# Zeros on TensorE in the first microseconds, one transfer for omega, and a place in the queue for the weight sums

## The chip, the cores and the metric

The kernel runs on one core of a Trainium2 chip. The metric is the device time of one execution in microseconds (us), as the median of three runs; lower is better. One further execution was recorded by the hardware profiler, and all rows below come from it.

## The reference

The program is random-feature attention, followed by two feed-forward blocks.

```python
def phi(x):                     # x: (4, 8, 576, 64), omega: (128, 64)
    h = einsum('bhsd,md->bhsm', x * scale, omega) - sum(x*x)/2
    return exp(h - max(h)) / sqrt(128)
q_p, k_p = phi(q), phi(k)
kv, z = einsum('bhsm,bhsd->bhmd', k_p, v), sum(k_p over s)
attn = (q_p @ kv) / (q_p @ z + 1e-6)          # -> x: (2304, 512)
y = ((x @ w_a) * (x @ w_b)) @ w_out           # 512 -> 1536 -> 512
out = maximum(y @ w_in, 0)**2 @ w_out2        # 512 -> 2048 -> 512
```

Inside `phi`, the term with the sum of squares is the same for every feature of a row and drops out against the maximum, so the kernel does not compute it.

## The kernel before

**Stages.** The prologue loads omega twice over, one copy above the other, turns it through TensorE against an identity matrix (`ident`), scales it and keeps it as `OMZ` and `OM`. Then *lanes* of small steps make the attention of the first 512 rows, batch 0, heads in pairs: a transfer brings a pair's rows (`kn` for k, `qn` for q), TensorE turns them (`ps_t`), ScalarE copies them out (`S`), TensorE multiplies with `OMZ` (`ps_p`), VectorE takes the extreme of each row (`nm`), ScalarE exponentiates (`kp`, `qp`). For k the result meets `V` on TensorE (`ps_kv`); for q it is turned once more (`ps_qt`), multiplied with the sums (`ps_n`), divided (`den`, `xh`) and turned into the columns of `x`. Rows 512 to 575 of each batch are called tails (`kt`, `qt`, `VT`, `ps_kt`). In fp32 each product of the program stands as two matmul records in the trace.

From about 40 us on the first feed-forward block runs in nine *passes* over blocks of 256 tokens. Passes 0 to 5 handle one block and half of the twelve 128-wide slices `f` of the hidden layer each (`PASSES`), with operands of 256 columns; passes 6, 7 and 8 handle two blocks and all slices, 512 columns at once, and are called wide. For each `f` a pass yields three units: product a (`wa`), product b (`wb`), and the output product (`y`) of an earlier slice. After product b the gate is formed: ScalarE scales a into `a_s`, VectorE multiplies b in, ScalarE casts the high part to fp32r and VectorE subtracts it from `a_s` for the low part; the two go to `gs` in narrow passes and to `g_mid` in wide passes 6 and 7. Between units the rest of the attention goes on as side lanes (`SIDES`).

**The weight sums.** Passes 6 and 7 take their later slices in pairs, by a Strassen-like scheme with seven products (`sP`, `sR`) for eight (`pair`). It needs sums of the weights: the generator `t_made(f)` (L282) adds the two parts of slice f's weights over 1,024 columns (`full`), makes four differences of 256 columns, and cuts each of the four results in a high part (ScalarE) and a low part (VectorE), in a `cut` tile, of which there are two. A transfer on SyncE's queue puts each `cut` into `t_d` in DRAM, from where `t_load` fetches it as `tsum` or `tz`. Ten slices are made, 6 to 11 and then 2 to 5, one step of the generator per unit of pass 6 (`t_work`).

**What sets the order.** The program is traced in the order in which it is written, and a scheduler then sets each engine's queue in advance: an instruction may go up the queue when its inputs and its memory are ready earlier. `tc.issue_after(x)` keeps what is traced in its block behind x in the queue of x's engine, without any wait for x to finish. Each engine works its queue strictly in order, so an instruction that waits holds up all behind it. Because of the scheduler's freedom, sums that pass 6 asks for can stand in the queues far ahead of pass 6.

`tail_turn` (L399) with `phi_wide` (L409) is the path of the tails; `load_split` and `step` cut the weights into parts, and `later_n` counts steps until one put-off part is issued.

## Time and profile before

| | us |
|---|---|
| median of 3 runs | 977.52 |
| lowest and highest run | 977.36, 978.56 |
| the profiled execution | 979.28 |
| its span, first to last instruction | 977.2 |

The profiled execution is 1.76 us over the median, and 2.1 us of it lie around the span. The profile gives, for each engine, when it was busy, when it was idle and what ended the idle time. TensorE appears as PE (matmuls) and PEld (weight loads), VectorE as DVE, ScalarE as ACT, GpSimd as POOL, and the queue on which SyncE issues transfers as SPq. A row of the timeline gives the start, the time to the end of the last of its instructions, and their number. The column PEclk is the granted share of TensorE's clock; it reads 1.00 in all windows shown, the first one included, and whether matmuls of one form take the same time in two stretches has to be read from their durations.

### The profile page before, as it was taken

How to read it: one execution, taken by the hardware profiler on the slowest of the kernel's cores; microseconds unless marked ns; L12 is line 12 of the kernel's file. 1: busy time of each engine (PE TensorE's matmuls, PEld its weight loads, DVE VectorE, ACT ScalarE, POOL GpSimd, SP SyncE). 2: the span in 40 equal slices, each digit the busy share in tenths (PEclk: the TensorE clock that was granted, in tenths of full speed). 3: DMA queues.
4: the chain of work that ended last, by engine and by line, in shares of the span. 5: the costliest groups of instructions: out<-in, count | busy, mean ns of one | idle time of the engine just before them, and what ended most of it. 6: DMA issues, size and time to landing. Idle time of an engine off the chain costs nothing.

```text
span 977.2 us, 18208 instructions
## 1 busy us (share of the span) xinstructions
PE 961.5 (98%) x6625; PEld 898.0 (92%) x6625; DVE 728.8 (75%) x1688; ACT 551.5 (56%) x1310; POOL 28.8 (3%) x54
## 2 busy tenths in 40 slices
PE   7999999999999999999999999999999999999998
PEld 6799998999998889889998888899999999999998
DVE  3888689887787865565456989789787347988794
ACT  5876566666655643253433544677676565555561
POOL 4000100000000000000000000000000000000000
PEclk9999999999999999999999999999999999999999
DMA  8656976655775365346547989246666869944301
GB/s 207 208 176 204 307 234 212 226 179 182 218 213 167 130 199 171 113 153 188 170 143 254 350 304 339 66 160 207 216 227 220 317 250 357 390 135 146 115 17 50
DMA packets 121961, 198.39 MB, mean 203 GB/s; under 512 B 28944, under 2 KB 84752, under 8 KB 119440
## 3 DMA queue, kind: packets, MB, share of 16 engines
q1 hardware_dynamic: 120336, 195.65, 60.5%
q0 software_dynamic: 1536, 1.58, 0.6%
q8 instruction: 53, 0.87, 0.4%
q14 instruction: 36, 0.29, 0.1%
HBM read 136.90 MB, written 60.29 MB: 202 GB/s over the span
## 4 chain that ended last, share of the span: by engine, by line
PE 81%; DVE 7%; DMA 5%; ACT 4%; issue 2%; SPq 0%; DVEq 0%; ACTq 0%
PE y L811 13%; PE abw L786 9%; PE oY L1478 8%; PE pY L1294 7%; PE ab L786 7%; PE oX L1478 5%; PE oW L1478 5%; PE sP L919 5%; PE pW L1294 4%; PE sR L919 3%; PE ps_n L638 3%; PE ps_kv L571 3%; PE ps_p L415 3%; PE ps_p L490 2%; DMA raw<-in_moe_w_b_dram 2%; PE ps_qt L628 2%
## 5 line engine op out<-in xcount | busy, mean ns | idle before, releaser
L786 PE MATMUL abw<-x_all,W 128*128 128x512 f32 x432 | 104.1, 392 | 0.0
L786 PEld LDWEIGHTS abw<-x_all,W 128*128 128x128 f32 x432 | 80.0, 188 | 15.7
L786 PE MATMUL ab<-x_all,W 128*128 128x256 f32 x576 | 84.9, 290 | 0.4 <-ACT W L226 0.4
L786 PEld LDWEIGHTS ab<-x_all,W 128*128 128x128 f32 x576 | 74.0, 189 | 1.7 <-ACT W L226 0.6
L811 PE MATMUL y<-g_mid,wo 128*128 128x512 f32 x288 | 75.1, 401 | 0.0
L811 PE MATMUL y<-gs,wo 128*128 128x256 f32 x432 | 66.5, 290 | 0.0
L811 PEld LDWEIGHTS y<-g_mid,wo 128*128 128x128 f32 x288 | 51.9, 188 | 10.1
L811 PEld LDWEIGHTS y<-gs,wo 128*128 128x128 f32 x432 | 56.6, 189 | 1.0 <-DVE wo L227 0.2
L1294 PE MATMUL pY<-W,M 128*128 128x384 f32 x228 | 44.1, 336 | 0.4 <-ACT F L1312 0.4
L499 ACT COPY c<-ps_p 128x256 f32<-128x256 f32 x76 | 27.7, 372 | 28.6 <-PE ps_p L490 28.1
L501 DVE CUSTOM_DVE_ANT_0 c<-ps_p,c 128x128 f32<-128x128 f32 x152 | 38.2, 285 | 7.5 <-ACT c L499 6.8
L786 PE MATMUL ab<-x,W 128*128 128x256 f32 x288 | 42.5, 288 | 0.0
L1442 ACT CAST W<-F 128x384 fp32r<-128x384 f32 x57 | 29.1, 513 | 22.9 <-PE oX L1478 11.0
L1478 PE MATMUL oX<-W 128*128 128x256 f32 x351 | 41.9, 276 | 0.0
L1478 PEld LDWEIGHTS oX<-W 128*128 128x128 f32 x351 | 40.8, 188 | 0.0
L1294 PEld LDWEIGHTS pY<-W,M 128*128 128x128 f32 x228 | 39.8, 188 | 1.0 <-ACT F L1312 0.9
L1320 ACT ACTIVATE F<-F 128x384 f32<-128x384 f32 x48 | 24.7, 518 | 26.9 <-DVE F L1315 26.7
L1478 PE MATMUL oY<-W 128*128 128x256 f32 x315 | 38.6, 277 | 0.0
L786 PEld LDWEIGHTS ab<-x,W 128*128 128x128 f32 x288 | 37.6, 191 | 0.1
L506 ACT ACTIVATE qp<-c,nm 128x128 f32<-128x128 f32 x88 | 31.0, 397 | 11.3 <-DVE nm L501 10.8
L1478 PEld LDWEIGHTS oY<-W 128*128 128x128 f32 x315 | 37.1, 188 | 0.0
L419 DVE TENSOR_REDUCE nm<-ps_p 128x4 f32<-128x512 f32 (+1 forms) x44 | 24.7, 564 | 14.9 <-PE ps_p L415 14.7
(287 smaller groups left out, 2408.7 us busy)
## 6 DMA issues: line engine op xcount, KB each, us to landing
wo<-wo_d SPq DMA_DIRECT2D x60, 512.0 KB, 3.9
s_d<-F SPq DMA_DIRECT2D x24, 768.0 KB, 4.7
tsum<-t_d SPq DMA_DIRECT2D x26, 512.0 KB, 4.0
t_d<-cut SPq DMA_DIRECT2D x40, 256.0 KB, 2.9
raw<-in_moe_w_out_dram SPq DMA_DIRECT2D x32, 256.0 KB, 5.2
raw<-in_moe_w_in_dram SPq DMA_DIRECT2D x16, 512.0 KB, 6.4
raw<-in_moe_w_a_dram SPq DMA_DIRECT2D x12, 512.0 KB, 3.8
raw<-in_moe_w_b_dram SPq DMA_DIRECT2D x12, 512.0 KB, 5.8
```

Of the source, the lines that this page charges most:

```text
L415: state["proj"] = nc.tensor.matmul(ps[:, 2 * x:2 * x + 2].rearrange("p h m -> p (h m)"), lhsT=s, rhs=OMZ.rearrange("p h m -> p (h m)"), st ...
L499: nc.scalar.copy(out=c, in_=ps[:, :, 1, :])
L501: nc.vector.tensor_tensor_reduce(out=c[:, x, :], in0=ps[:, x, 0, :], in1=c[:, x, :], scale=1.0, scalar=3.0e38, op0=ALU.add, op1=ALU.min, a ...
L506: nc.scalar.activation(out=dst[:, 2 * n + x, :], in_=c[:, x, :], func=ACTF.Exp, scale=-1.0, bias=nm[:, x:x + 1],)
L571: lambda h=h, j=j: nc.tensor.matmul(ps[:, h, :], lhsT=kp[:, 4 * h + j, :], rhs=V2[h][:, j] if odd else V[:, j, h, :], start=(j == j0), sto ...
L638: lambda x=x: nc.tensor.matmul(pn[:, x, :], lhsT=t["qT"][:, x % 2 * len(g) + x // 2, :], rhs=kv[:, x % 2, :], start=True, stop=True,)
L786: nc.tensor.matmul(ps, lhsT=wv[:, s_, kc, :], rhs=x[..., kc, m_, :], start=(kc == 0 and (s_, m_) == TERMS[0]), stop=(kc == KC - 1 and (s_, ...
L811: nc.tensor.matmul(y_part(pi, f, c), lhsT=wo[pi, f][:, s_, c * 128:(c + 1) * 128], rhs=g[:, m_, :],  start=(f == f0 and (wide or c % 2 == ...
L919: nc.tensor.matmul(ps[:, z], lhsT=b(z, s_, kk), rhs=a[:, kk, m_, :], start=(first and z == 0 and kk == 0 and (s_, m_) == TERMS[0]), stop=( ...
L1294: nc.tensor.matmul(ps[c][:, x, 0:TH], lhsT=w[:, s_, 128 * kk:128 * kk + 128], rhs=y[:, ai, kk, m_, :], start=((c, x) not in seen and kk == ...
L1442: ahead_of["cast"] = nc.scalar.copy(out=sop[:, 0], in_=src)
L1478: nc.tensor.matmul(tiles_of(p, t), lhsT=sops[n][:, s_, 128 * t:128 * t + 128], rhs=w[:, m_, :], start=(fresh and k == 0 and (t % 2 == 0 or ...
```

## The change

In the prologue, VectorE clears `OMZ` before `V` and `VT`, and casts it into the last 256 columns of the weight area `W`, where it serves as a block of zeros. `fill(n)` issues n matmuls of 128x256 zeros into a bank that nothing reads (`blank`): 8 ahead of omega's turning, 6 behind it, and 4 behind the turning of the first k rows. The first `ps_p` products are queued behind these. Omega comes by one transfer that reads it twice. The first tail's turning moves behind the second product of the first k rows. Every weight sum is queued behind the most recent gate: the addition of `full` behind the gate's VectorE subtraction, the casts into `cut` behind its ScalarE cast. So that the most recent gate is known, the wide passes now record it in `state["g"]` too. One put-off part of the first weights goes one step later (`later_n`).

```diff
@@ -239,7 +239,7 @@
         return state["g"][0] if at == "g" else at and state[at]
 
     waiting = []
-    later_parts, later_n = [], [9]
+    later_parts, later_n = [], [10]
     CAST_BEHIND = {("a", 6): "cast", ("a", 7): "S", ("a", 10): "g", ("a", 1): "S"}
     APART = {("a", 6), ("a", 10)}
 
@@ -285,10 +285,11 @@
 
         w = seg("W", 8192 * f, 2, 2, 512)
         full = top["full"].tile([128, 4, 256], F32, tag="full", name="full")
-        nc.vector.tensor_tensor(
-            out=full.rearrange("p (a r) n -> p a (r n)", a=2), in0=f32(w[:, :, 0]),
-            in1=f32(w[:, :, 1]), op=ALU.add,
-        )
+        with tc.issue_after(state["g"][1].ins):
+            nc.vector.tensor_tensor(
+                out=full.rearrange("p (a r) n -> p a (r n)", a=2), in0=f32(w[:, :, 0]),
+                in1=f32(w[:, :, 1]), op=ALU.add,
+            )
         yield
         for o, x, y in ((0, 2, 0), (2, 3, 2), (3, 3, 0), (1, 1, 3)):
             nc.vector.tensor_tensor(
@@ -298,7 +299,8 @@
             cuts = []
             for x in (n, n + 1):
                 c = top["cut"].tile([128, 2, 256], F32, tag="cut", name="cut")
-                nc.scalar.copy(out=c[:, 0].bitcast(F32R), in_=full[:, x])
+                with tc.issue_after(state["g"][0].ins):
+                    nc.scalar.copy(out=c[:, 0].bitcast(F32R), in_=full[:, x])
                 nc.vector.tensor_tensor(
                     out=c[:, 1].bitcast(F32R), in0=full[:, x], in1=c[:, 0], op=ALU.subtract
                 )
@@ -355,6 +357,16 @@
             for fn in fns[-2::-1]:
                 fn()
 
+    zero = area["W"][:, FA * 2048 - 256:FA * 2048]
+    blank = bank(7, [128, 512], "blank")[:, 0:256]
+
+    def fill(n):
+
+        for _ in range(n):
+            state["fill"] = nc.tensor.matmul(
+                blank, lhsT=zero[:, 0:128], rhs=zero, start=True, stop=True,
+            )
+
     def prologue():
         warm = ap2.tile([128, 1], F32, tag="den", name="warm", bufs=3)
         nc.vector.memset(warm, 0.0)
@@ -362,17 +374,23 @@
         make_identity(nc, ident)
         for t in V2:
             nc.scalar.copy(out=t[:, :, D:D + 1], in_=warm.unsqueeze(1).to_broadcast([128, 4, 1]))
-        nc.sync.dma_start(out=om[:, 0, :], in_=omega)
-        nc.sync.dma_start(out=om[:, 1, :], in_=omega)
-
-
-        nc.vector.memset(V, 1.0)
-        nc.vector.memset(VT, 1.0)
+        nc.sync.dma_start(out=om, in_=omega.unsqueeze(1).to_broadcast([M, 2, D]))
+
+
+        nc.vector.memset(OMZ, 0.0)
+        t = nc.vector.tensor_copy(out=zero, in_=OMZ.rearrange("p a m -> p (a m)"))
+        with tc.issue_after(t.ins):
+            t = nc.vector.memset(V, 1.0)
+        with tc.issue_after(t.ins):
+            nc.vector.memset(VT, 1.0)
         nc.vector.memset(VT[64:128, :, :, 0, :], 0.0)
         nc.vector.memset(VT[0:64, :, :, 1, :], 0.0)
-        nc.vector.memset(OMZ, 0.0)
+        fill(8)
         ps = at_bank([128, M], "ps_om")
-        nc.tensor.transpose(ps, om.rearrange("p a d -> p (a d)"), ident)
+        with tc.issue_after(state["fill"].ins):
+            t = nc.tensor.transpose(ps, om.rearrange("p a d -> p (a d)"), ident)
+        with tc.issue_after(t.ins):
+            fill(6)
 
         nc.scalar.mul(out=OMS, in_=ps, mul=-SCALE)
         for x in range(2):
@@ -411,11 +429,12 @@
         n = 2 * len(rows)
         nm = ap2.tile([128, n], F32, tag="nm", name="nm", bufs=4)
         ps = at_bank([128, n, M], "ps_p")
-        for x, s in enumerate(rows):
-            state["proj"] = nc.tensor.matmul(
-                ps[:, 2 * x:2 * x + 2].rearrange("p h m -> p (h m)"), lhsT=s,
-                rhs=OMZ.rearrange("p h m -> p (h m)"), start=True, stop=True,
-            )
+        with tc.issue_after(state["fill"].ins) if "proj" not in state else nullcontext():
+            for x, s in enumerate(rows):
+                state["proj"] = nc.tensor.matmul(
+                    ps[:, 2 * x:2 * x + 2].rearrange("p h m -> p (h m)"), lhsT=s,
+                    rhs=OMZ.rearrange("p h m -> p (h m)"), start=True, stop=True,
+                )
         nc.vector.tensor_reduce(out=nm, in_=ps, axis=AXX, op=ALU.min)
         for x in range(n):
             state["exp"] = nc.scalar.activation(
@@ -461,6 +480,12 @@
                 with tc.issue_after(state["proj"].ins):
                     for c in cols:
                         nc.tensor.transpose(ps[:, c], nat[:, c], ident)
+            elif "k" in self.at:
+                with tc.issue_after(state["fill"].ins):
+                    for c in cols:
+                        t = nc.tensor.transpose(ps[:, c], nat[:, c], ident)
+                with tc.issue_after(t.ins):
+                    fill(4)
             else:
                 together([lambda c=c: nc.tensor.transpose(ps[:, c], nat[:, c], ident) for c in cols])
             if self.wide:
@@ -525,7 +550,12 @@
                         in_=v[b, h0:h0 + 2, SM:S, :].rearrange("h t d -> t h d"),
                     )
         yield
-        st = tail_turn("k", b, g)
+        if state["n"] < 4:
+            yield
+            with tc.issue_after(state["proj"].ins):
+                st = tail_turn("k", b, g)
+        else:
+            st = tail_turn("k", b, g)
         yield
         yield
         kp = ap2.tile([128, 2, M], F32, tag="qp", name="kpt", bufs=2)
@@ -959,8 +989,7 @@
             outs(*pending.pop(0))
             g = top["g"].rearrange("p z h (t n) -> p t z h n", t=2)
             for t, e in enumerate((e1, e5)):
-                nc.scalar.copy(out=g[:, t, :, 0], in_=e)
-                nc.vector.tensor_tensor(
+                state["g"] = nc.scalar.copy(out=g[:, t, :, 0], in_=e), nc.vector.tensor_tensor(
                     out=g[:, t, :, 1], in0=e, in1=f32(g[:, t, :, 0]), op=ALU.subtract
                 )
             for z in range(2):
@@ -1041,8 +1070,7 @@
                 if len(pending) > 1:
                     outs(*pending.pop(0))
                 for c, a_s in a_ss:
-                    nc.scalar.copy(out=g[:, 0, c], in_=a_s)
-                    nc.vector.tensor_tensor(
+                    state["g"] = nc.scalar.copy(out=g[:, 0, c], in_=a_s), nc.vector.tensor_tensor(
                         out=g[:, 1, c], in0=a_s, in1=f32(g[:, 0, c]), op=ALU.subtract
                     )
                 for _ in range(2):
```

TensorE's queue at the program's start, before: omega's turning, the first k rows, the products with `OMZ`, the tail's turning (`ps_tt`).

```order
L375 MATMUL ps_om<-ident,om 128x128
L465 MATMUL ps_t_177<-ident,kn 128x128 x4
L415 MATMUL ps_p<-OMZ,S 128x256
L403 MATMUL ps_tt<-ident,kt 128x128
L415 MATMUL ps_p<-OMZ,S 128x256 x3
L415 MATMUL ps_p<-OMZ,T 128x256
```

The same place in the changed kernel:

```order
L366 MATMUL blank<-W 128x256 x8
L391 MATMUL ps_om<-ident,om 128x128
L366 MATMUL blank<-W 128x256 x6
L486 MATMUL ps_t_192<-ident,kn 128x128 x4
L366 MATMUL blank<-W 128x256 x4
L434 MATMUL ps_p<-OMZ,S 128x256 x2
L421 MATMUL ps_tt<-ident,kt 128x128
L434 MATMUL ps_p<-OMZ,S 128x256 x2
L434 MATMUL ps_p<-OMZ,T 128x256
```

Eighteen matmuls are new, and `ps_tt` stands one product later; the products themselves keep their order.

VectorE's queue in pass 3, where the first of the ten weight sums stands before (`c,nm`, `qT` and `den` belong to side lanes):

```order
L501 ISA c,nm<-ps_p,c 128x128
L501 ISA nm 128x1
L633 COPY qT<-ps_qt 128x512
L288 TENSOR_TENSOR full<-W 128x1024
L609 TENSOR_SCALAR den<-ps_n 128x4
```

The same place now:

```order
L526 ISA c,nm<-ps_p,c 128x128
L526 ISA nm 128x1
L663 COPY qT<-ps_qt 128x512
L1092 TENSOR_TENSOR a_s<-ab,a_s 128x256
L526 ISA c,nm<-ps_p,c 128x128
L526 ISA nm 128x1
L639 TENSOR_SCALAR den<-ps_n 128x4
```

The 1,024-column addition is gone from here, and the gate's multiplication (`a_s`) comes up. VectorE's queue in the changed kernel between two gates of pass 6, a place where no such row stood before in this number:

```order
L1093 TENSOR_TENSOR g_mid<-a_s,g_mid 128x256
L1092 TENSOR_TENSOR a_s<-abw,a_s 128x256
L295 TENSOR_TENSOR full<-full 128x256
L639 TENSOR_SCALAR den<-ps_n 128x4
L295 TENSOR_TENSOR full<-full 128x256
L1093 TENSOR_TENSOR g_mid<-a_s,g_mid 128x256
L295 TENSOR_TENSOR full<-full 128x256
L304 TENSOR_TENSOR cut<-full,cut 128x256
L295 TENSOR_TENSOR full<-full 128x256
L642 RECIPROCAL den<-den 128x4
```

All ten additions of `full` now stand here, behind the last gate of pass 5; before, seven of the ten stood ahead of the first gate of pass 6.

## Rows read from the trace of the kernel before

**Rows 1.** The page's first part: busy time, share of span, instructions.
```profile
PE 961.5 (98%) x6625; PEld 898.0 (92%) x6625; DVE 728.8 (75%) x1688; ACT 551.5 (56%) x1310; POOL 28.8 (3%) x54
```

**Rows 2.** Timeline of the start: start us, us, engine, line, instruction, count, idle before.
```profile
0.95 0.49 DVE L369 MEMSET V<- 128x520 f32 x1
1.19 0.42 SPq L366 DMA_DIRECT2D om<-in_omega_dram  x1
1.65 0.43 SPq L441 DMA_DIRECT2D kn<-in_k_dram  x1
...
5.00 1.11 PE L465 MATMUL ps_t<-ident,kn 128*128 128x128 f32 x4 [1.54 <-DMA kn<-in_k_dram]
...
6.15 0.58 ACT L468 COPY S<-ps_t 128x512 f32<-128x512 f32 x1 [1.62 <-PE ps_t L465]
...
6.79 1.22 PE L415 MATMUL ps_p<-OMZ,S 128*128 128x256 f32 x2 [0.68 <-ACT S L468]
...
8.02 2.77 PE L415 MATMUL ps_p<-OMZ,S 128*128 128x256 f32 x6
...
9.11 0.69 DVE L419 TENSOR_REDUCE nm<-ps_p 128x4 f32<-128x512 f32 x1 [4.25 <-PE ps_p L415]
...
9.84 1.14 ACT L421 ACTIVATE kp<-ps_p,nm 128x128 f32<-128x128 f32 x4 [1.31 <-DVE nm L419]
...
11.54 1.14 ACT L421 ACTIVATE kp<-ps_p,nm 128x128 f32<-128x128 f32 x4 [0.57 <-DVE nm L419]
...
12.50 0.51 PE L571 MATMUL ps_kv<-V,kp 128*128 128x65 f32 x2
12.56 0.64 ACT L421 ACTIVATE kpt<-ps_p,nm 128x128 f32<-128x128 f32 x2
...
12.96 0.34 PE L571 MATMUL ps_kv<-V,kp 128*128 128x65 f32 x2
...
14.57 0.87 ACT L468 COPY S<-ps_t 128x256 f32<-128x256 f32 x2
15.00 2.43 PE L415 MATMUL ps_p<-OMZ,S 128*128 128x256 f32 x10
```

**Rows 3.** Windows: stretch, length, busy time (instructions) by engine, PEclk, DMA share, GB/s.
```profile
core 0: us, PE busy (x) PEld busy (x) DVE busy (x) ACT busy (x) POOL busy (x), PEclk, DMA share, GB/s
0.00:15.00 15.00, 9.64 (x42) 7.74 (x42) 3.97 (x10) 7.01 (x23) 7.75 (x18) 1.00 0.91 230
34.00:42.00 8.00, 7.25 (x52) 6.12 (x50) 7.74 (x14) 7.62 (x21) 0.00 (x0) 1.00 0.84 263
160.00:180.00 20.00, 19.77 (x161) 18.81 (x160) 18.66 (x57) 12.40 (x33) 0.00 (x0) 1.00 0.69 228
175.00:287.00 112.00, 110.91 (x917) 107.23 (x917) 90.19 (x346) 75.38 (x233) 4.67 (x8) 1.00 0.66 202
287.00:404.00 117.00, 115.61 (x716) 99.85 (x716) 80.97 (x259) 54.52 (x160) 2.32 (x4) 1.00 0.52 168
```

**Rows 4.** Chain of waits: start us, us, what; a paired product, two sum transfers.
```profile
189.31 6.10 DMA t_d<-cut
...
295.53 4.15 DMA t_d<-cut
...
359.86 1.42 PE sP L919 x12
```

**Rows 5.** The sums' instructions: duration ns min/median/max, first and last start us.
```profile
L294 DVE TENSOR_TENSOR full<-full x40: 405/419/427, 180.6 to 330.7; 128x256 f32<-128x256 f32 x40
L301 ACT CAST cut<-full x40: 388/407/418, 181.8 to 339.4; 128x256 fp32r<-128x256 f32 x40
L302 DVE TENSOR_TENSOR cut<-full,cut x40: 404/419/426, 185.0 to 342.2; 128x256 fp32r<-128x256 f32 x40
L288 DVE TENSOR_TENSOR full<-W x10: 1216/1222/1226, 175.9 to 327.0; 128x1024 f32<-128x1024 f32 x10
```

**Rows 6.** The transfers of the sums (L308), from issue to landing.
```profile
DMA to landing us min/median/max: 2.0/2.9/6.1
```

## The prediction

> **What bounds the kernel now.** I read the page first, then windows of the stages that the change touches, then the timeline of the start, then the chain of waits. The page shows TensorE busy for 961.5 us of a span of 977.2 us, while VectorE has 728.8 us and ScalarE 551.5 us [rows 1]. So only 15.7 us of TensorE's time are idle, and a change can win in three ways: fewer idle microseconds, matmuls that take less time, or fewer matmuls. This change removes no matmul and adds eighteen. The windows say where idle time is [rows 3]: 5.4 us of the first 15 (15.00 less 9.64), 1.1 us of the 112 between 175 and 287 us (the end of the narrow passes, where seven of the ten weight sums are made), and 1.4 us of the 117 between 287 and 404 us (pass 6). The reader is to see that the start alone holds a third of all idle time.
>
> The timeline shows that the start is slow in a second way [rows 2]. The six matmul records at 8.02 us take 2.77 us, 0.46 each; ten records of the same form at 15.00 us take 2.43 us, 0.24 each. The pair of `ps_kv` at 12.50 us takes 0.51 us, the pair at 12.96 us 0.34. So TensorE runs at about half rate until some 12.7 us and then at full rate; I read the two as its levels of 1.2 and 2.4 GHz. The column of the granted clock does not tell them apart, since it reads 1.00 in the first window as everywhere [rows 3]. Before the rise TensorE had worked without a break since 6.79 us, after an idle gap of 0.68 us, that is for 5.9 us.
>
> **Part 1: zeros and omega.** VectorE's first large step, the clearing of `V`, starts at 0.95 us and takes 0.49 us for 520 columns [rows 2], so clearing 256 columns of `OMZ` takes some 0.25 us. The cast of 256 columns has no row; the nearest is a subtraction of 256 columns at 0.42 us [rows 5], which I take as its upper end. So the zeros are there at 0.95 + 0.25 + 0.42 = 1.6 us. A fill of 256 fp32r columns at full rate takes 1.42 us / 12 = 0.12 us [rows 4], at half rate 0.23. Eight end at 1.6 + 1.9 = 3.5 us. Omega is turned behind them, later than now, but is only needed by the first product at 6.79 us, which covers it with about 3 us. Six more fills end near 5.1 us. The first k rows land about 0.4 us sooner, since one transfer issue of 0.42 us ahead of theirs is gone; TensorE reaches them at 5.1 us at the soonest, against 5.00 now. The last four fills take 0.9 us beside a copy to `S` of 0.58 us, so at half rate they hold the first product by up to 0.3 us, at full rate by nothing. I put the first product at 6.9 us: a loss of 0.1, bounds 0 and 0.3.
>
> What comes back is the half rate behind it. If TensorE works without a break from 1.6 us and its clock rises after as long a stretch as now, it rises at 1.6 + 5.9 = 7.5 us in place of 12.7. I walk the chain of the first k rows on from there, first as if the clock were up by the first product. Two products are four records, 0.97 us; the reduction, which started at 9.11 us, starts near 7.9; it takes 0.69, and the exponentials of 1.14 us run from 8.6 to 9.8. The second reduction hides beside them. The next two sets of exponentials (1.14 and 0.64 us) are ScalarE's own work and end near 11.5, against 13.20 now (12.56 + 0.64). ScalarE then has a gap of 1.37 us before the next copies to `S` at 14.57 us, in which it mostly waits for `ps_kv` matmuls at half rate; at full rate they are nearly done when the last exponentials are. I leave 0.4 us of the gap, and after half of the 0.87 us of copies the next products start at 12.4 us, where they start at 15.00 now: 2.6 us sooner. With the whole gap left it is 1.7. With the clock up only at 7.5, 0.6 us of half rate stays ahead of the reduction, worth 0.3; together with the 0.1 above I take **2.2 us**.
>
> The Trainium skill, page "TensorE: Matmul & The Clock Gate", section "HAM oscillation — how this bites in real kernels", prices a slow stretch at half its length. By that rule the 5.9 us would be worth 3.0 us, and the total 0.8 us lower than mine; in this trace the exponentials of ScalarE lie between, and they do not get shorter. The same page, section "What's actually happening", says that the moment of the rise changes from run to run of one kernel; the three runs here differ by 1.2 us, which does not speak against it, and one profile cannot show it.
>
> From 15 us on every queue keeps its order up to pass 3, and transfers are issued as buffers come free, so the lead should be carried on. What would be late next is a transfer: in the first 15 us the DMA engines are busy at a share of 0.91 [rows 3], and the third load of k rows now stands behind the load of the output weights on SyncE's queue. That could take back some tenths. `ps_tt` and the put-off part of the first weights move by one step and cost nothing, since the two products and the exponentials cover them.
>
> **Part 2: weight sums.** One slice costs VectorE 1.22 + 4 x 0.419 + 4 x 0.419 = 4.57 us and ScalarE 4 x 0.407 = 1.63 us [rows 5]. Seven slices leave the stretch of 175 to 287 us: 32 us of VectorE's 90.2 and 11 us of ScalarE's 75.4. They go to the stretch of 287 to 404 us, where VectorE comes from 81.0 to some 110 or 113 of 117 us, 94 to 97%, and ScalarE from 54.5 to 66.
>
> In the first stretch TensorE is idle for 1.1 us in all. One idle wait there follows a transfer of a sum of 6.10 us [rows 4], for which ScalarE stands until a `cut` tile is free. The gain lies between 0 and 1.1 us; I take 0.7, since VectorE falls to about half load.
>
> In pass 6 behind a waiting sum stand gates, features and turned columns, on which TensorE's next products wait. Two rows bound the price of so full a VectorE [rows 3]. Between 160 and 180 us it is 93% busy, ScalarE 62%, and TensorE is idle for 0.23 of 20 us, 1.2%; in 117 us that is 1.4, what pass 6 has now. Between 34 and 42 us VectorE is 97% busy, ScalarE 95%, and TensorE is idle for 0.75 of 8 us, 9.4%; that would be 11.0 us, 9.6 more. Pass 6 would have ScalarE at 56%, so the first row is nearer. I take 2.0%, 2.3 us, 0.9 more than now. The sums' transfers bound it too: a slice needs two rounds of cast, subtraction and transfer, 0.41 + 0.42 + 2.9 us at the median, 7.5 us in 11.7 us per slice; at the longest transfer of 6.1 us [rows 6] it would be 13.9 and not fit.
>
> Part 2 thus costs 0.9 - 0.7 = **0.2 us**, bounds -1.1 and +9.6.
>
> **The sum.** Against the profiled execution: 979.28 - 2.2 + 0.2 = 977.3 us. That execution lies 1.76 us over the median of the three runs, so the median comes to 975.5 us. What a measurement of this kernel can tell from no change is about 0.2%, 2 us: this forecast lies just outside it, at 975.57 the line.
>
> **The rivals.**
> *The start gives little.* The zeros are cleared and cast later than I put them, or matmuls of zeros do not bring the clock up, and the rise moves only to where the real products bring it. For it: TensorE did other work from 5.00 us now, too, and that did not bring the rise before 12.7. Against it: nothing but gaps tells those 1.8 us apart from the later work. With a third of the gain, 0.8, and 0.2 for part 2, it is 976.9 us; with none, 977.8. Chance 0.24, on the side of no difference.
> *VectorE bounds pass 6.* The place is VectorE's queue between two gates, where the sums now stand; the mechanism is that a cast waits for a `cut` tile, VectorE for the cast, and the gate behind it for both. For it: 94 to 97% of load, and the transfers of 4.15 and 6.10 us in the chain of waits [rows 4]. Against it: 160 to 180 us. At the rate of the stretch from 34 to 42 us it costs 9.6, and the time is 977.52 - 2.2 - 0.7 + 9.6 = 984.2 us. It decides for slower from an extra idle time of 4.9 us in pass 6 on, 5.4% of it in all. Chance 0.16.
> *Both parts give all.* The start gives the 3.0 us of a slow stretch halved, the narrow passes 0.9, pass 6 costs nothing: 973.6 us. Chance 0.12.
>
> **How the numbers follow.** My forecast has the remaining 0.48, with its own range from 974.4 to 976.4; about 0.10 of it lies above 975.57. Faster: 0.38 + 0.12 = 0.50. No difference: 0.24 + 0.10 = 0.34. Slower: 0.16. For a range that holds 8 in 10 I go from 973.2, just under the best case, to 979.4, which takes in the first rival and a pass 6 that costs up to some 5 us; the worse part of the second rival is left out.
>
> **What would show it.** In the changed profile the records of the first `ps_p` products should take about 0.24 us each, the ten-record group of 15.00 us should start near 12.8 us (15.00 less 2.2), and pass 3 to 5 should have less idle TensorE time than 1.1 us. Pass 6 should show VectorE over 90% busy and TensorE idle for 2 to 3 us; 6 us or more would prove the second rival. If the first products still take 0.46 us per record, part 1 is wrong. If the lead at 15 us is there but gone by 47 us, a transfer took it back.

## The result, and the profile after

The changed kernel took 990.75 us in the median of four runs (988.24 to 991.68), beside 977.76 us for the kernel before: a ratio of 1.0117, with a 95% interval of 1.0102 to 1.0131. It is slower by about 13 us; I had forecast 2 us faster. A second measurement, beside the experiments, gave 986.96 against 978.07 us, 1.0095 [1.0078, 1.0112]. The loss is thus some 9 to 13 us. The profiled execution took 988.24 us, 8.96 more than that of before, and all places below come from it. It is the quickest of the four, so the profile can account for 9 of the 13 us and not for the rest.

The page's first part answers to [rows 1]: VectorE and ScalarE have the work that they had, and TensorE is busy for 6.7 us more.

```profile
PE 968.2 (98%) x6643; PEld 899.6 (91%) x6643; DVE 728.9 (74%) x1689; ACT 552.3 (56%) x1310; POOL 28.9 (3%) x54
```

The start, in the timeline of the changed kernel, answers to [rows 2] (start us, us, engine, line, instruction, count, idle before).

```profile
1.21 0.29 DVE L381 CAST W<-OMZ 128x256 fp32r<-128x256 f32 x1
...
1.56 2.08 PE L366 MATMUL blank<-W 128*128 128x256 f32 x8 [1.56 <-DVE W L381]
...
6.35 1.13 PE L434 MATMUL ps_p<-OMZ,S 128*128 128x256 f32 x4 [0.20 <-ACT S L493]
...
7.52 0.69 DVE L438 TENSOR_REDUCE nm<-ps_p 128x4 f32<-128x512 f32 x1 [2.27 <-PE ps_p L434]
...
11.71 2.43 PE L434 MATMUL ps_p<-OMZ,S 128*128 128x256 f32 x10
```

The reader is to see two things. The first four records of `ps_p` take 1.13 us, 0.28 each, where they took 0.46: TensorE is at its faster level from the first product on. And the ten records that started at 15.00 us start at 11.71, 3.3 us sooner. The start did what was asked of it. One profile overstates how much: in the twelve profiles, this one and those of the experiments, that have the eighteen fills, this group starts between 11.52 and 12.50 us, and in e2, which has the old start, at 14.08.

The windows answer to [rows 3] (stretch, length, busy time and number of instructions by engine, granted clock, DMA share, GB/s). The last line, of 345 to 404 us, is the later half of the line above it.

```profile
0.00:15.00 15.00, 13.11 (x76) 11.59 (x76) 6.03 (x15) 8.94 (x30) 8.96 (x20) 1.00 0.86 227
34.00:42.00 8.00, 7.36 (x54) 6.51 (x54) 7.23 (x15) 7.05 (x19) 0.00 (x0) 1.00 0.65 221
160.00:180.00 20.00, 19.78 (x158) 18.69 (x156) 16.26 (x55) 12.70 (x35) 0.00 (x0) 1.00 0.79 257
175.00:287.00 112.00, 111.39 (x895) 105.89 (x895) 67.11 (x283) 65.97 (x203) 4.68 (x8) 1.00 0.49 144
287.00:404.00 117.00, 112.00 (x681) 95.47 (x680) 95.70 (x290) 61.28 (x175) 2.33 (x4) 1.00 0.61 196
345.00:404.00 59.00, 54.12 (x371) 47.39 (x370) 49.92 (x140) 27.54 (x76) 2.33 (x4) 1.00 0.76 232
```

The same 59 us in the kernel before:

```profile
345.00:404.00 59.00, 58.79 (x412) 52.47 (x411) 34.44 (x110) 21.40 (x62) 2.32 (x4) 1.00 0.57 180
```

VectorE and ScalarE are relieved between 175 and 287 us as expected (90.2 to 67.1, 75.4 to 66.0). Between 345 and 404 us TensorE has 371 records where it had 412, and is idle for 4.9 us where it was for 0.2. The number of records is the better measure here: it fell by 10%, the busy time by 8%, since in the profile records overlap and a longer step from one start to the next need not show as idle time.

To see where the time goes over the whole program I compared, record by record, when the 5,400 main matmuls of the two feed-forward blocks start. The table gives the difference to the profiled execution of before (us, minus is sooner), at four places named by before's time, and beside it how long ScalarE's casts waited for the transfer of a `cut` tile (`t_d<-cut`), how many did, and TensorE's records between 345 and 404 us. In e10 and e11 the casts are GpSimd's.

| kernel | 40 us | 333 us | 438 us | last | casts waited (number) | records 345:404 |
|---|---|---|---|---|---|---|
| before | | | | | 2.3 (5) | 412 |
| changed | -2.7 | -4.5 | +6.0 | +9.6 | 15.0 (9) | 371 |
| e1 start alone | -2.5 | +0.3 | +0.3 | +0.9 | 4.0 (5) | 411 |
| e2 ties alone | -0.9 | +0.7 | +9.6 | +8.6 | 13.5 (8) | 374 |
| e3 no wait | -2.8 | +0.1 | -0.1 | +0.2 | none | 412 |
| e4 no differences | -2.3 | -1.1 | +3.0 | +2.1 | 10.8 (12) | 385 |
| e5 change again | -2.6 | -3.7 | +5.7 | +8.1 | 16.8 (11) | 375 |
| e6 last five tied | -2.5 | -2.9 | +1.2 | +1.9 | 10.0 (7) | 388 |
| e7 last two tied | -2.5 | -0.3 | -0.3 | +1.0 | 4.5 (6) | 411 |
| e8 half tiles | -2.5 | -3.3 | +3.4 | +7.3 | none by this name | 385 |
| e9 no zeros | -1.6 | -2.0 | -1.9 | -2.7 | 3.2 (4) | 412 |
| e10 GpSimd cuts | -2.0 | +1.0 | +10.1 | +10.3 | 17.7 (13) | 353 |
| e11 GpSimd sums | -2.5 | +12.9 | +12.2 | +12.2 | 18.9 (13) | 395 |
| e12 no wait, its order | -2.9 | -4.3 | +1.8 | +4.9 | none | 395 |
| e13 wait, e3's order | -2.1 | +11.7 | +41.9 | +42.7 | 34.2 (15) | 268 |

The changed kernel is 4.5 us ahead at 333 us and 6.0 behind at 438, a difference of 10.5 us. Not all of it is lost time. In five kernels (changed, e2, e5, e8 and e12) 22 records of side lanes, 16 of them of `ps_kv`, stand behind the product of 333 us, where the other kernels have them ahead of it. In the kernel before these 22 take 2.3 us. The records of `ps_kv` up to this product, before and changed (windows as above, of `ps_kv` alone):

```profile
288.00:333.10 45.10, 3.79 (x32) 3.80 (x32) 0.29 (x1) 0.27 (x1) 1.00 0.50 165
286.00:328.60 42.60, 1.96 (x16) 1.86 (x16) 0.00 (x0) 0.27 (x1) 1.00 0.48 164
```

So the true lead at 333 us is 2.2 us, and the changed kernel loses 8.2 us in the second half of pass 6 and shortly behind. At 438 us all kernels have the same records behind them. For the five kernels, 2.3 us is taken off wherever a loss between 333 and 438 us is named below. Another 3.6 us go in the second block; there the kernels drift by -1.0 to +3.9 us, and I take no meaning from it.

What TensorE waits for there, in the changed kernel between 287 and 430 us (line, waited for, us, times, longest; before has no wait of over 0.8 us in this stretch):

```profile
PE ps_x L681 <- DVE xh L643: 1.3, 1, 1.3
PE sP L949 <- ACT ge L960: 1.2, 2, 0.9
PE ps_qt L658 <- ACT qp L531: 1.0, 1, 1.0
PE sP L949 <- DMA tsum<-t_d: 0.9, 1, 0.9
PE y L841 <- ACT g_mid L992: 0.6, 1, 0.6
```

How the first two come about is in the chain of waits of the changed kernel (start us, us, what), which answers to [rows 4]:

```profile
354.83 5.63 DMA t_d<-cut
360.92 0.42 DVE cut L304
361.47 0.43 DVE xh L643
362.04 0.42 PE ps_x L681 x2
...
366.82 5.01 DMA t_d<-cut
372.28 0.59 ACT ge L960
372.92 0.63 PE sP L949 x3
```

Read the second piece together with ScalarE's timeline:

```profile
370.63 0.26 ACT L470 CAST S<-ps_t 64x128 fp32r<-64x128 f32 x1
371.86 0.40 ACT L303 CAST cut<-full 128x256 fp32r<-128x256 f32 x1 [0.96 <-DMA t_d<-cut]
372.28 0.59 ACT L960 COPY ge<-sP 128x512 f32<-128x512 f32 x1
```

A `cut` tile is sent at 366.82 and lands after 5.01 us. ScalarE is done with its other work at 370.9 and stands, for 0.96 us, at a cast that needs that tile. Behind the cast stands `ge`, the copy that empties a bank of TensorE's, and behind `ge` wait the next `sP` products. In the first piece the cast stands for 4.3 us, VectorE's subtraction behind it, and the features (`xh`) behind that.

The transfers themselves became slower where the sums now are. The sums' transfers in the whole program land in 3.0 us at the median, against 2.9 in [rows 6], but the twenty between 345 and 404 us take 3.9:

```profile
DMA to landing us min/median/max: 2.0/3.9/6.6
```

There they share the DMA engines with the loads of pass 6: the share went from 0.57 to 0.76.

### The profile page after: what moved, and what is told of

It reads as the page before. It is cut to its first block, busy times and chain, and to the rows that moved or that the text cites. A ratio compares the mean times of both kernels' runs of the same rounds, so it can differ in the third digit from the quotient of the medians.

```text
span 986.4 us, 18274 instructions
## 1 busy us (share of the span) xinstructions
PE 968.2 (98%) x6643; PEld 899.6 (91%) x6643; DVE 728.9 (74%) x1689; ACT 552.3 (56%) x1310; POOL 28.9 (3%) x54
## 4 chain that ended last, share of the span: by engine, by line
PE 76%; DMA 9%; DVE 8%; ACT 4%; issue 2%; SPq 0%; DVEq 0%; ACTq 0%
PE y L841 12%; PE abw L816 10%; PE ab L816 8%; PE oY L1506 7%; PE pY L1322 6%; PE oX L1506 4%; PE oW L1506 4%; PE sP L949 3%; PE pW L1322 3%; DMA t_d<-cut 3%; PE ps_n L668 2%; PE sR L949 2%; PE ps_kv L601 2%; PE ps_p L515 2%; PE ps_p L434 2%
## 5 line engine op out<-in xcount | busy, mean ns | idle before, releaser
L841 PE MATMUL y<-g_mid,wo 128*128 128x512 f32 x288 | 77.1, 402 | 0.6 <-ACT g_mid L992 0.6
L841 PEld LDWEIGHTS y<-g_mid,wo 128*128 128x128 f32 x288 | 51.5, 189 | 10.3 <-ACT g_mid L992 1.0
L1470 ACT CAST W<-F 128x384 fp32r<-128x384 f32 x57 | 29.1, 513 | 22.9 <-PE oX L1506 10.5
L1506 PE MATMUL oX<-W 128*128 128x256 f32 x351 | 41.9, 276 | 0.0
L1471 DVE TENSOR_TENSOR W<-F,W 128x384 fp32r<-128x384 f32 x57 | 30.9, 552 | 6.3 <-ACT W L1470 5.8
```

The costliest lines, as they stand in the source:

```text
L841: nc.tensor.matmul(y_part(pi, f, c), lhsT=wo[pi, f][:, s_, c * 128:(c + 1) * 128], rhs=g[:, m_, :],  start=(f == f0 and (wide or c % 2 == ...
L1470: ahead_of["cast"] = nc.scalar.copy(out=sop[:, 0], in_=src)
L1471: ahead_of["rest"] = nc.vector.tensor_tensor(out=sop[:, 1], in0=src, in1=f32(sop[:, 0]), op=ALU.subtract)
L1506: nc.tensor.matmul(tiles_of(p, t), lhsT=sops[n][:, s_, 128 * t:128 * t + 128], rhs=w[:, m_, :], start=(fresh and k == 0 and (t % 2 == 0 or ...
```

## The experiments

All ran beside the kernel before on the same chip, in four groups (e1 to e4, e5 to e8, e9 to e11, e12 and e13).

### e1 and e2: each part alone

e1 is the changed kernel without the two ties of the sums; e2 is the kernel before with nothing but the ties.

```diff
-        with tc.issue_after(state["g"][1].ins):
-            nc.vector.tensor_tensor(
+        nc.vector.tensor_tensor(
...
-                with tc.issue_after(state["g"][0].ins):
-                    nc.scalar.copy(out=c[:, 0].bitcast(F32R), in_=full[:, x])
+                nc.scalar.copy(out=c[:, 0].bitcast(F32R), in_=full[:, x])
```

> Part 1 alone: zeros, one transfer for omega, order of the prologue; the weight sums are free to go up the queues as before, and all queues read as in the kernel before but for the prologue. In the profile of the changed kernel the first product of pass 0 started 2.67 us sooner than before and the lead grew to 3.3 us by 172 us, the end of what is common. Theory A (the whole loss comes from the ties of the sums): the lead stays to the end, 974.5 to 975.5 us, ratio 0.9967 to 0.998, and the wait of 1.3 us of the second block's products at 694 us is not there. Rival B (the shift of all transfers by one place on their queues, or another effect of part 1, slows later stages, the second block among them): 977 to 981 us, with late gaps in the second block as in the changed kernel.

> Part 2 alone: only the ties of the weight sums, with the prologue of before. Theory A: it costs what the changed kernel lost plus the lead that it had, about 13 + 3 = 16 us, so 992 to 995 us; the gaps of TensorE lie between 345 and 415 us. Rival B (both parts cost): 985 to 989 us.

Measured: e1 977.41 against 978.40 us, ratio 0.9994 [0.9982, 1.0006]; e2 986.31 us, 1.0079 [1.0059, 1.0098]. The start alone loses nothing, and the ties alone lose 7.9 us. The parts add up to 1.0073, near the 1.0095 of e5 and below the first 1.0117; what is left over, 2 to 4 us, stands in neither part. By their times both runs fall in the ranges of rival B, not in those of theory A. But B's mechanism does not show: e1's profile is at +0.3 us at 438 us and at +0.9 at the end. What failed in A is that the lead stays: the start, though 2.5 us ahead at 40 us, shows less than 1 us in the median.

### e3: no cast waits for a transfer

The transfers into `t_d` read the weights instead of the `cut` tiles, so the sums are computed but not sent, and a `cut` tile is free as soon as it is written. They also stand behind the latest load of the output weights on SyncE's queue.

```diff
-                nc.sync.dma_start(out=t_d[f // 2 - 1][:, x, f % 2], in_=c)
+                with tc.issue_after(state["wo"].ins):
+                    nc.sync.dma_start(
+                        out=t_d[f // 2 - 1][:, x, f % 2],
+                        in_=f32(w[:, x // 2, :, 256 * (x % 2):256 * (x % 2) + 256]),
+                    )
```

> The changed kernel, but the 40 transfers of the sums read the weights themselves in place of the cut tiles, behind the loads of the output weights on the queue; the sums computed are not stored, so pass 6 and 7 take other weights. Bytes and number of transfers stay, and the sums' work on VectorE and ScalarE stays; only no cast waits for a transfer any more. Theory T (the round of cast, subtraction and transfer with two cut tiles holds ScalarE and, behind it, VectorE): most of the loss of pass 6 goes, 977 to 981 us. Rival L (VectorE is simply too full in pass 6): 986 to 991 us, as the changed kernel.

Measured: 978.4 us, 0.9999 [0.9987, 1.001]. The loss is gone. Its window between 345 and 404 us:

```profile
345.00:404.00 59.00, 58.83 (x412) 53.06 (x411) 51.86 (x155) 28.73 (x82) 2.33 (x4) 1.00 0.86 269
```

VectorE is busier than in the changed kernel (51.86 of 59 us, 88%) and the DMA engines too (0.86), and TensorE is idle for 0.2 us. So neither VectorE's load nor the share of the DMA engines is the cause by itself. In this run the sums' work is harmless; but the scheduler had also set another order, which e12 and e13 tell apart from the wait.

### e4: less of VectorE's work

The forty differences of 256 columns are left out; the rounds of cast, subtraction and transfer stay.

```diff
-        for o, x, y in ((0, 2, 0), (2, 3, 2), (3, 3, 0), (1, 1, 3)):
+        for o, x, y in ():
```

> The changed kernel without the four differences of each weight sum (40 VectorE instructions of 0.42 us, 16.8 us), so other weights are stored; casts, subtractions and transfers stay. Rival L (load of VectorE): VectorE falls to some 80% in pass 6 and most of the loss goes, 978 to 982 us. Theory T (the round through the transfer): the round stays, and the loss with it, 985 to 990 us.

Measured: 982.15 us, 1.0041 [1.0027, 1.0055]. 17 us of VectorE's work fewer take back about half, and the time lies just above the range of rival L and below that of theory T. The ten runs fall in two groups, five from 980.28 to 980.76 and five from 983.54 to 984.66, with the median between them; the profile is of the lower group. The casts wait for transfers for 10.8 us instead of 13.5 to 16.8. The order of the queues is another one here too, so this run cannot say whether the work or the order took back the half.

### e5, e6 and e7: the change again, and fewer slices tied

e5 is the changed kernel. In e6 the ties hold for the last five slices only, in e7 for the last two; the others go back to where the kernel before makes them.

```diff
-        with tc.issue_after(state["g"][1].ins):
+        with tc.issue_after(state["g"][1].ins) if f in (11, 2, 3, 4, 5) else nullcontext():
```

> The whole change once more, beside before on the chip of the three kernels that follow. The parts alone were measured against before at a ratio of 0.9994 (the start) and 1.0079 (the ties). Theory A, the parts add and the 13.0 us of the first measurement belong to the chip or to where transfers fell in those runs: some 7 us over before, ratio 1.006 to 1.009. Theory B, the earlier start makes the rounds of pass 6 fall worse: some 13 us again, ratio 1.011 to 1.014.

> Only the last five of the ten slices stay tied; the first five are made where the kernel before makes them (175 to 250 us). From 345 us on every engine then has the same sums to do as in the changed kernel, ahead of it five fewer. Theory A, a round of cast, subtraction and transfer is what costs, and it costs where the transfers share the DMA engines with the loads of pass 6 (345 to 404 us, DMA share 0.76): the loss stays whole, within 2 us of the changed kernel on the same chip. Theory B, it is VectorE's and ScalarE's work in pass 6 as a sum, or the order from 287 us on: with five of ten slices back, about half of the loss, some 4 to 6 us over before.

> Only the last two slices stay tied; eight are made where the kernel before makes them. In the changed kernel five slices stand between 345 and 404 us, in before none, here two. Theory A, each slice there costs its rounds (some 10.5 us for five, 2.1 us each): some 3 to 5 us over before. Theory B, the cost begins only when ScalarE's queue is filled by one round behind the other: two slices have room, under 1 us over before.

Measured: e5 986.96 us, 1.0095 [1.0078, 1.0112]; e6 980.91, 1.0031 [1.0018, 1.0045]; e7 978.69, 1.0002 [0.9989, 1.0014]. Of e5's two theories the parts roughly add (A), a little over A's upper end of 1.009. For e6 neither fits: five slices still stand between 338 and 387 us, but a third of the loss is left, less than B's half too. e7 is B's: two slices have room. (The 10.5 us of its theory A holds the 2.3 us of moved records.) Two slices cost next to nothing, and the cost begins between two and five: by the medians it is 0.6, 2.8 and 8.9 us for two, five and ten tied slices, by the profiles 0.0, 4.1 and 7.0 us between 333 and 438 us. Whether it then grows faster than the number of slices stays open, as the medians say yes and the profiles no. The casts' waits for transfers go the same way, 4.5, 10.0 and 16.8 us, from 2.3 in the kernel before.

### e8: four smaller cut tiles

A `cut` tile holds the high half alone, so that four fit in the place of two; the low half is written over the sum, and both are sent.

```diff
-                c = top["cut"].tile([128, 2, 256], F32, tag="cut", name="cut")
+                c = top["cut"].tile([128, 256], F32, tag="cut", name="cut")
...
-                    out=c[:, 1].bitcast(F32R), in0=full[:, x], in1=c[:, 0], op=ALU.subtract
+                    out=full[:, x].bitcast(F32R), in0=full[:, x], in1=c, op=ALU.subtract
```

> The changed kernel, but a cut tile holds the high half alone (1 KB per partition), so that four fit where two did; the low half is left in the place of the sum itself and both are sent from there, in two transfers of half the size. The planner then sets a few rows of every queue in another order (about one in ten). Theory A, a cast stands because both cut tiles wait for their transfer: with four tiles most of the loss goes, 0 to 3 us over before. Theory B, it is the number and bytes of the transfers in 345 to 404 us, or the work: the loss stays at 7 to 13 us, or grows with the twice as many issues.

Measured: 984.67 us, 1.0068 [1.0049, 1.0086], 6.6 us over before. No cast waits for the transfer of a `cut` tile any more (by the profile three casts wait for 1.9 us in all for loads, and VectorE twice, 1.3 us, for the transfer of a `full`), and three quarters of e5's loss are still there, just under theory B's 7. Not all of it is the sums': TensorE's granted clock fell here, which it does nowhere in the changed kernel's pass 6.

```profile
366.00:368.00 2.00, 1.52 (x12) 1.29 (x12) 2.00 (x6) 1.52 (x4) 0.00 (x0) 1.00 0.95 229
368.00:372.00 4.00, 3.27 (x19) 2.96 (x19) 3.76 (x13) 1.85 (x6) 0.00 (x0) 0.79 0.88 298
372.00:376.00 4.00, 4.00 (x26) 3.61 (x26) 2.36 (x6) 2.62 (x8) 0.00 (x0) 0.79 0.61 186
```

A mean of 0.79 over 8 us loses 1.7 us of work at the full clock; ahead of it TensorE was idle for 0.5 of 2 us, and for 0.7 of the 4 us in which it fell. That leaves 2.7 of the 4.4 us that e8 loses between 333 and 438 us. The runs say the same in another way: two of the four, 982.51 and 983.48 us, had a mean granted clock of 0.999 and 1.000, against 0.998 in the other two, and they are still 4.4 and 5.4 us over before. So the wait for the tile is not the whole cause, and in e3 something else had gone with it.

### e9: one fill of zeros

The start alone, as in e1, with one fill in place of eighteen.

```diff
-        fill(8)
+        fill(1)
...
-            fill(6)
+            pass
```

> The start of the changed kernel with one fill of zeros in place of eighteen, and no ties: omega by one transfer, the first k rows ahead, clearing and casting in the new order. Beside the start with all its fills (977.41 us, ratio 0.9994, clock's rise at 6.94 us in its profile) it gives the price of the zeros alone. Theory A, zeros bring the clock up and nothing else does: its rise comes some 6 us after the first work that stays, at 10 to 13 us, the second set of ps_p products stands some 1.5 to 2.5 us later than with the fills, and the whole is within 1 us of before all the same, since the lead is lost behind 40 us. Theory B, the lead is kept in the median and was hidden by chance: then it is 1 to 2 us slower than the start with its fills.

Measured: 977.18 against 978.05 us, 0.9994 [0.9985, 1.0003]: as with all fills. Its timeline:

```profile
6.20 2.07 PE L432 MATMUL ps_p<-OMZ,S 128*128 128x256 f32 x4 [0.68 <-ACT S L489]
...
8.28 1.91 PE L432 MATMUL ps_p<-OMZ,S 128*128 128x256 f32 x4
...
13.44 2.42 PE L432 MATMUL ps_p<-OMZ,S 128*128 128x256 f32 x10
```

Without the zeros the first two groups of four take 2.07 and 1.91 us, half rate, where the changed kernel took 1.13. Zeros do bring the clock up sooner: the traces' record of the granted clock, which begins with the rise, has it at 10.21 us here and between 4.82 and 7.68 us in the twelve profiles with all fills. That is worth 13.44 - 12.13 (e1's row of ten records) = 1.3 us at this place, a little under theory A's 1.5, and 0.9 to 1.9 us by the twelve. The other 1.6 us of e9's lead over [rows 2] are not the zeros'. At the end the two kernels are alike.

### e10 and e11: the rounds on GpSimd

e10 is the changed kernel with the casts and the subtractions on GpSimd; e11 is the start alone with all of a sum on GpSimd.

```diff
-                    nc.scalar.copy(out=c[:, 0].bitcast(F32R), in_=full[:, x])
-                nc.vector.tensor_tensor(
+                    nc.gpsimd.tensor_copy(out=c[:, 0].bitcast(F32R), in_=full[:, x])
+                nc.gpsimd.tensor_tensor(
```

> The changed kernel, but the casts and the subtractions into the cut tiles are GpSimd's, which has next to nothing else to do; the sums and differences stay on VectorE behind the gates. Then no queue that TensorE waits for stands behind a cut tile whose transfer has not landed. Theory A, that standing is the cost: in 345 to 404 us TensorE is idle for under 1.5 us (the changed kernel: 4.9 and 4.5) and the whole is 0 to 3 us over before. Theory B, VectorE's work between the gates or the transfers' share of the DMA engines is the cost: some 4 to 9 us over before, since the sums and differences (2.9 us a slice) and all bytes are as they were.

> The start of the changed kernel without ties, with everything of a weight sum (sum, differences, casts, subtractions) on GpSimd: VectorE loses 2.94 us and ScalarE 1.63 us a slice, and neither waits for a transfer of a sum. If waits for those rounds are what eats the earlier start between 175 and 345 us (1.5 us of its lead went there), the lead of 1.5 to 2.5 us stays to the end: ratio 0.997 to 0.999. If it goes to the loads of weights at 47 to 70 us and to chance, nothing is gained: 0.999 to 1.001. If GpSimd is so slow that the sums are late for pass 6, or slows VectorE, it is slower.

Measured: e10 988.86 us, 1.0112 [1.0092, 1.0133]; e11 989.75 us, 1.012 [1.0106, 1.0134]. I had thought that with GpSimd no queue that matters would stand behind a `cut` tile. Both kernels show where that was wrong. In e10 VectorE stands at the next addition (waits of VectorE, 287 to 430 us: line, waited for, us, times, longest):

```profile
DVE full L289 <- POOL cut L304: 7.4, 5, 3.4
```

`full` has one buffer, so the next sum cannot begin before the last cut of the one before is made, and that waits for its transfer as it did. VectorE also became slower beside GpSimd: the 40 differences took 485 ns at the mean, where the changed kernel took 419.

```profile
L295 DVE TENSOR_TENSOR full<-full 128x256 f32<-128x256 f32 x40 | 19.4, 485 | 0.5
```

In e11 SyncE's queue stands (its waits, 230 to 310 us), and with it the loads behind a `t_d` transfer; TensorE waits for those loads (260 to 310 us):

```profile
SPq L308 <- POOL cut L302: 35.9, 14, 5.9
SPq L308 <- POOL cut L301: 17.6, 5, 6.4
```

```profile
PE y L839 <- DMA wo<-wo_d: 4.6, 2, 3.5
PE ps_kv L599 <- DMA V<-in_v_dram: 2.5, 1, 2.5
```

Two things go together in e11, and no run parts them. A round that is moved to another engine still holds every in-order queue that has an end of it. And GpSimd is slow at it: a slice takes 10.2 us of it (102.2 us for ten), against 4.57 us of VectorE and 1.63 of ScalarE, so the cuts are late by themselves, the third outcome that was expected. The Trainium skill, page "Perfetto Trace Analysis", section "Optimizing Scalar/DVE Operations", says that giving work to ScalarE or even GpSimd may make sense where VectorE is saturated, and that between VectorE and GpSimd it might not help; in these two runs it did not.

### e12 and e13: the wait and the order, told apart

e3 took the wait away, but the scheduler then also set the queues in another order: some 4% of TensorE's rows, 7% of VectorE's and 6% of ScalarE's stand elsewhere. So e12 is e3 with the queues of TensorE, VectorE, ScalarE and SyncE held in the changed kernel's order, and e13 is the changed kernel with the queues of TensorE, VectorE and ScalarE held in e3's. Both chain each engine's instructions by a table of their names:

```diff
+    for table in ORDER.values():
+        row = [f"I-{x}" for x in table.split()]
...
+        for a, b in zip(row, row[1:]):
+            tc.add_manual_dep(
+                MADE[b], a,
+                mybir.DependencyInfo(mybir.DependencyClass.NoSync, mybir.DependencyReason.DATA),
```

> The kernel e3_store_from_w (the transfers of the sums read the weights themselves, the sums are computed and not sent, so no cast waits for a transfer) lost nothing, but the planner had also set its queues in another order than those of the changed kernel. Here the queues of TensorE, VectorE, ScalarE and SyncE are held, row by row, in the order of the changed kernel. Theory A, the wait for the transfer is the cost: the loss is gone in this order too, 0 to 2 us over before. Theory B, the order in which sums, casts and gates stand is the cost: the loss stays, 7 to 13 us over before.

> The other half of the same comparison: the changed kernel with all its sums, casts and transfers of cut tiles, but with the queues of TensorE, VectorE and ScalarE held in the order of e3_store_from_w. Theory A, the wait for the transfer is the cost: the loss stays whatever the order, 7 to 15 us over before, and ScalarE's casts wait for transfers for some 17 us between 287 and 430 us. Theory B, it is the order: 0 to 2 us over before.

Measured: e12 985.58 against 977.88 us, 1.0073 [1.0057, 1.0089]; e13 1019.21 us, 1.0416 [1.0398, 1.0433]. Theory A fails for e12 and theory B for e13, so neither holds alone; e13 also lies far beyond A's 15 us. In the changed kernel's order, half of the loss or more is there without any wait of a cast for a transfer: 7.7 of 8.9 us by the medians, 3.8 of 7.0 us between 333 and 438 us by the profiles of e12 and e5. (e12's profiled execution is its quickest, 983.56 us at a mean granted clock of 1.000; the other three have 0.997 to 0.999, so some of the 7.7 us can be clock.) In e3's order, the waits cost 41 us, of which some 17 are clock: the granted clock had a mean of 0.983 over the span of 1,019.5 us. ScalarE's waits between 287 and 430 us, first the changed kernel's, then e12's, then e13's:

```profile
ACT cut L303 <- DMA t_d<-cut: 15.0, 9, 4.3
ACT cut L303 <- DVE full L295: 9.7, 7, 2.3
```

```profile
ACT cut L1808 <- DVE full L1808: 10.3, 8, 2.3
```

```profile
ACT cut L1804 <- DMA t_d<-cut: 31.0, 14, 4.2
```

(In these two kernels all instructions carry the line of the table; tiles tell them apart.) In the changed kernel's order the casts stand singly among ScalarE's copies (38 groups of 40 casts, against 23 in e3) and the differences singly among VectorE's gates (40 groups, against 33). A cast that has no transfer to wait for then waits for VectorE's next difference, as it did in the changed kernel for 9.7 us, and the copies behind it wait with it. What TensorE waits for in e12 over the same stretch:

```profile
PE ps_qt L1808 <- ACT qp L1808: 1.0, 1, 1.0
PE sP L1808 <- DMA tsum<-t_d: 0.8, 1, 0.8
PE y L1808 <- ACT g_mid L1808: 0.6, 1, 0.6
PE sP L1808 <- ACT ge L1808: 0.2, 1, 0.2
```

Beside the changed kernel's list, the wait for `xh` is gone and that for `ge` nearly so: these are the two pieces of the chain in which a cast stood for its tile. The waits for `qp`, for the load of a sum (`tsum`) and for `g_mid` are as they were: these belong to the order. In e3's order a slice's casts stand closer together; that went with no loss where tiles were free at once, and with the greatest where each cast needs a landed transfer. That the closeness of the casts is what matters is not shown: e8 has them in 23 groups too, and lost.

## Why the prediction was wrong

**What bounds the kernel** was right: TensorE, with a third of its idle time in the start.

**Part 1, the zeros and omega.** The times of the steps held or came sooner: the zeros were there at 1.5 us (1.6 foretold), the clock rose at 5.23 (7.5 foretold; 4.82 to 7.68 in the twelve profiles with this start), the first product came at 6.35 (6.9), in the four records at 0.28 us each. The ten-record group came at 11.71, 3.3 us sooner than in the profile before, where I had 2.2, between 1.7 and 2.6. Against e2's start, 14.08, it is 2.4 us, so 2.2 was about right there. The price by the Trainium skill's rule, 3.0, lies between the two. Two steps behind it failed. The first is "the lead should be carried on". In e1's profiled execution the 2.5 us were gone by 333 us, over a load at 54 us of 6.8 us and the sums' transfers, whose pieces in its chain are

```profile
243.93 4.22 DMA t_d<-cut
...
261.33 6.15 DMA t_d<-cut
...
291.40 3.08 DMA t_d<-cut
...
295.46 4.44 DMA t_d<-cut
```

In e9's profiled execution the chain has one such piece (259.38 us, 6.20), 2.0 us of lead were left at 333 us, and it ended 2.7 us ahead. The ratios of e1 and e9 both say -0.6 us, and both intervals (to 0.9982 and 0.9985, 1.8 and 1.5 us) exclude the 2.2. The runs of one kernel spread over 4 to 5 us (before: 976.16 to 980.82), so whether a run keeps the lead is decided anew each time by how transfers land; that is argued from two profiles, not shown. The second is the step that took [rows 2] for the start of before as such. e2, whose start is before's, has the ten records at 14.08 us, not 15.00. About 0.9 us of the gain was one late execution. The Trainium skill, page "TensorE: Matmul & The Clock Gate", section "What's actually happening", says that the clock's rise moves from run to run; these two executions of one start agree with that (rise at 12.87 us in before, at 11.29 in e2), as do the two of the changed kernel (5.23 and, in e5, 7.49).

**Part 2, the weight sums.** This is the term that decided: foretold at +0.2 us, measured at +7.9 us (e2), inside the bound of +9.6. The 0.7 us of the narrow passes did not show: TensorE's idle time there fell from 1.1 to 0.6 us, but the lead shrank from 3.3 us at 164 us to 1.6 at 292. It was 2.2 at 333 us, where the chain of before runs through the transfer of 4.15 us [rows 4] and that of the changed kernel does not. Pass 6 was foretold at +0.9; from 292 to 438 us it lost 6.4 us in e2 and 7.6 in the changed kernel, and in its second half alone 6.6 and 8.2. The failed step is the sentence that "the first row is nearer", the 160 to 180 us of [rows 3], and with it the reading of VectorE's busy share as what prices the stretch. The idle share between 345 and 404 us was 8.3% (4.9 of 59 us), close to the 9.4% of 34 to 42 us, with VectorE busy for 85% and ScalarE for 47%; in e3 VectorE at 88% cost nothing. The share of an engine's time says little about a stretch in which its instructions wait for one another.

The other step that failed is the one that let a round of 7.5 us fit in 11.7 us per slice. It compared a median with a mean, and set the longest transfer, with which the round would not fit, aside. The transfers landed in 3.9 us, not 2.9, and more to the point, a round does not have to exceed its slice to cost: each cast stands at one place of an in-order queue, and if its tile is 1 us late there, everything behind is 1 us late. I had also priced the round as time, and not as a constraint on the order: half of the loss or more (e12: 7.7 us, beside 8.9 in e5; by the profiles 3.8 beside 7.0 between 333 and 438 us) is in the order that the scheduler set under the ties, and the rest in the waits for transfers that this order leaves standing. That ten rounds and two tiles left it no better order is argued, not shown.

**The rivals.** "VectorE bounds pass 6" named the cast that waits for its tile, VectorE behind it and the gate behind both, and gave 984.2 us; that is the chain at 354.83 and 366.82 us. Its condition, VectorE 94 to 97% busy, did not come about (95.7 of 117 us, 82%), and the cost began at two to five tied slices. Its chance of 0.16 was far too small for a mechanism whose two transfers already stood in [rows 4]. "Both parts give all" was near the lead of the start in this one profile, and wrong about the time and about pass 6.

**What stays open.** Why the first measurement gave 13.0 us and the second 8.9: their intervals just overlap, and the profiles of both are near 9. How much of e12's loss is the interleaving of casts and differences, how much the late load of a sum, and how much other rows of that order: no run changes one of these alone. And a version clearly faster than the kernel before was not found; e1 and e9 lie within its spread.

## What to carry to other kernels

Before work is tied to a later place, count its rounds through buffers there (tiles, transfer time at that place, instructions that stand behind each wait), and not the share of time that its engines have free. A lead at the start is worth in the median only what transfers farther on do not take back, and its size cannot be read from one profile. When an experiment lets the scheduler choose a new order, hold the order in a second run before blaming the wait that was removed.

## What was not expected of the hardware

GpSimd is little slower than ScalarE in casting 256 columns (457 ns against 407 in [rows 5]), but takes twice VectorE's time for a subtraction (812 against 419). The Trainium skill, page "GPSIMD Engine Reference", section "4.1 Engine selection", has this factor of about two against VectorE for two inputs, and roughly the full rate for one. The rows agree on two inputs; for one, the one VectorE cast of this form that is shown (L381 above) took 0.29 us, so GpSimd's 457 ns are 1.6 times that. From e10's groups (line, engine, operation, form, count, busy us, mean ns, idle before):

```profile
L304 POOL TENSOR_TENSOR cut<-full,cut 128x256 fp32r<-128x256 f32 x40 | 32.4, 812 | 2.8
L303 POOL CAST cut<-full 128x256 fp32r<-128x256 f32 x40 | 18.2, 457 | 117.1 <-DMA V<-in_v_dram 54.8 <-DVE full L295 44.6 <-DMA t_d<-cut 17.7
```

VectorE's instructions can become longer while GpSimd works: e10's differences, with a mean of 485 ns, have a median of 424 and a longest of 836. A loss of TensorE's time can cost clock on top. In e13 the granted clock had a mean of 0.85 between 345 and 404 us, where TensorE was idle for 10.9 us:

```profile
345.00:404.00 59.00, 48.10 (x268) 42.04 (x268) 39.23 (x114) 22.66 (x64) 0.00 (x0) 0.85 0.48 156
```

The changed kernel, idle for 4.9 us of the same stretch, kept 1.00.
